# Windowed attention with sinks and a channel mix on one core: sink values as row tiles, 1 KB rows for q and k, longer filling, new orders

## The chip, the cores and the metric

The kernel runs on one core of one Trainium2 chip. The metric is the device time of one execution in microseconds; lower is better. A core has a matrix engine (TensorE, in profiles PE, with its weight loads shown as PEld), a vector engine (VectorE, DVE), an activation engine (ScalarE, ACT), a general engine (GpSimd, POOL) and SyncE (SP), which issues DMAs. Each engine works through its own queue in order and waits at semaphores for the others. Matmuls write to PSUM, in eight banks; everything else lies in SBUF, with 128 partitions.

## The reference, cut to what matters

Attention over 4 batches, 8 heads, 768 tokens and 64 elements per head, in which a query sees the first 4 tokens (the sinks) and the last 128, followed by a channel mix with squared ReLU and a sigmoid gate:

```python
scores = scale * np.matmul(q, k.transpose(0, 1, 3, 2))
keep = is_sink | in_window               # pos < 4, or 0 <= rel < 128
a = softmax(np.where(keep, scores, -1e9))
x = np.matmul(a, v)                      # heads side by side: B, S, 512
xk = mu_k * x + (1.0 - mu_k) * x_prev    # x_prev: one token earlier
xr = mu_r * x + (1.0 - mu_r) * x_prev
k = np.maximum(xk @ w_k, 0.0)            # 512 x 1024
v = k * k @ w_v                          # 1024 x 512
out = (1.0 / (1.0 + np.exp(-(xr @ w_r)))) * v
```

Inputs and output are float32.

## The kernel before, in words

The work is cut into 12 units of 256 tokens (4 batches, 3 units each; T is the unit's number in its batch). For each unit there are four stages.

`prepare` casts q and k to bf16 and transposes them, so that the 64 elements of a head lie on partitions (tiles qt and kt). One chunk c is a pair of heads, and a half is two chunks. For units in KD (k, from 4) and QD (q, from 8) SP issues a DMA transpose (L603); for the others PE transposes (L616) into a PSUM bank, and ACT or DVE evacuates it (L624). These "PE-transposed" units load q and k in rows of 512 B (L403: two neighbouring tokens of a head in one partition), a whole tensor of a unit by one DMA of 512 KB, for unit 0 by two of 256 KB. v, and q and k of the units transposed by DMA, are loaded in rows of 256 B (L386, L396). v is cast into vb, with a column of ones (L638). For the first unit of a batch `prepare` also gathers the sinks' keys (L655, ksink, on POOL) and the sinks' values (L661 on PE and L665 on DVE, vsink, in which row 32c + 4a + s has sink s for head a of chunk c).

`attend` has PE multiply keys by queries for two chunks at a time into the two tiles sc (L701, matmuls over 64 rows, the two heads of a chunk in the upper and the lower half of the array); ACT takes the exponential (L737, tile e); DVE sets what is out of the window to zero (L751). Scores against the sinks are one set of four matmuls of 32 columns each per unit (L678), their exponential is the tile es (L685), in which the four chunks lie on 32 partitions each. `values` (from L757) multiplies by v: for T > 0 and each group g of 128 tokens first one matmul es x vsink over 128 rows for both heads (L763, 128x130), then four of e x vb (L775, 128x65). A chunk's values lie in one PSUM bank. DVE takes the reciprocal of the sums (L788) and multiplies (L791, tile x).

`mix` transposes x on PE (L814), ACT or DVE evacuates it (L823, xt), DVE takes the difference to the token before (L841, td) and makes xk and xr (L852).

`ffn` of the unit before has PE multiply xk by w_k (L902, keys), ACT or DVE take the ReLU (L912, L916), DVE square it (L924, kk), PE multiply xr by w_r (L933), ACT take a tanh (L939), PE multiply kk by w_v (L951) and DVE join both (L960); SP stores (L967). The weights are loaded in float32 and cast (L552 to L558).

The order of the work is not left to a scheduler. The kernel first notes every operation in a list (`Plan.op`), with its engine, a cost, what it reads and writes and the buffers that it takes and holds. ORDER has the numbers of these operations for each engine, in the order in which that engine does them, and CHOICE names the engine for operations that may run on several. `Plan.schedule` walks these lists with the costs to assign buffers and to merge the engines; it also places zero matmuls (L971, on the tile `warm`) into the time in which PE has nothing to do by the plan's clock: where a gap is over 300 ns (600 ns before 4 us), a bank is free, and the plan's clock stands below `fill_until`, 22000 ns. In PSUM the pool "sc" has 2 tiles of two banks each and the pool "bank" has the other 4 banks. The plan allows 100 ns (SWITCH) where PE changes between kinds of tiling (mode 0 for the whole array, 1 for scores, 2 for sink scores); the cost of `values` is 358 ns for T > 0.

```python
for g in range(2):
    if T > 0:
        nc.tensor.matmul(out=o[:, g, :, :],
                         lhsT=buf["es", u][:, 128 * g:128 * g + 128],
                         rhs=vsink[b % 2][:, 2 * c:2 * c + 2, :],
                         start=True, stop=False, skip_group_check=True)
```

Of the kernel before, what the change touches and what calls it, by code (L numbers as in the profile page):

```python
# [18 lines left out]
    79: "ACT", 82: "ACT", 83: "ACT", 85: "ACT", 87: "ACT", 89: "DVE", 94: "DVE", 95:  # L19
    "DVE", 97: "DVE", 101: "DVE", 102: "DVE", 128: "DVE", 134: "DVE", 136: "DVE", 137:  # L20
    "DVE", 140: "ACT", 141: "DVE", 150: "DVE", 191: "DVE", 192: "ACT", 193: "ACT", 218:
    "DVE", 265: "DVE", 273: "DVE", 278: "DVE", 305: "DVE", 343: "DVE", 346: "DVE", 348:
    "DVE", 352: "ACT", 354: "DVE", 361: "DVE", 423: "DVE", 429: "ACT", 430: "ACT", 499:
    "DVE", 501: "DVE", 504: "DVE", 507: "DVE", 508: "ACT", 520: "DVE", 586: "ACT", 587:
    "ACT", 654: "DVE", 658: "DVE", 660: "DVE", 663: "DVE", 672: "DVE", 736: "DVE", 738:
    "ACT", 739: "DVE", 744: "DVE", 751: "DVE", 815: "DVE", 816: "ACT", 825: "DVE", 885:
    "DVE", 887: "DVE", 891: "ACT", 892: "ACT", 1003: "DVE",
# [13 lines left out]
TOGETHER = 2  # L41

SWITCH = 100.0
# [8 lines left out]
        90, 93, 106, 96, 99, 104, 117, 77, 109, 114, 132, 138, 142, 129, 125, 120, 156,  # L52
        135, 158, 149, 184, 190, 169, 236, 208, 209, 212, 213, 220, 221, 161, 166, 172,
        177, 216, 194, 181, 201, 217, 187, 238, 291, 299, 292, 295, 300, 303, 249, 304,
        226, 296, 241, 246, 307, 224, 228, 277, 232, 229, 252, 261, 233, 267, 257, 311,
        264, 284, 270, 312, 319, 344, 309, 315, 330, 316, 349, 367, 375, 368, 376, 322,
        371, 395, 327, 372, 333, 338, 397, 275, 353, 379, 360, 380, 383, 408, 385, 387,
        422, 388, 445, 453, 446, 454, 400, 427, 405, 475, 411, 416, 391, 431, 392, 457,
        438, 458, 449, 473, 486, 450, 463, 526, 530, 527, 531, 500, 538, 461, 505, 539,
        469, 510, 470, 554, 478, 483, 534, 494, 489, 535, 512, 565, 557, 465, 579, 466,  # L60
        542, 519, 544, 562, 550, 584, 573, 551, 588, 546, 568, 632, 602, 547, 603, 606,
        614, 607, 595, 630, 643, 615, 620, 610, 618, 611, 640, 635, 678, 682, 679, 683,
        664, 646, 690, 706, 708, 686, 651, 687, 691, 626, 671, 719, 711, 622, 627, 694,
        623, 761, 757, 765, 758, 762, 766, 722, 696, 741, 727, 716, 775, 785, 702, 750,
        769, 743, 770, 796, 703, 788, 793, 698, 773, 699, 817, 777, 781, 778, 782, 835,
        831, 839, 832, 836, 799, 840, 859, 861, 843, 804, 847, 844, 824, 855, 849, 869,
        864, 872, 856, 907, 915, 908, 851, 916, 852, 880, 875, 911, 893, 912, 919, 900,
        920, 935, 937, 923, 925, 931, 948, 932, 973, 940, 974, 981, 945, 982, 951, 977,
        959, 978, 956, 985, 927, 966, 986, 928, 991, 989, 1001, 1009, 1005, 1002, 1013,
        1006, 1014, 1010, 993, 1021, 997, 994, 998, 1017, 1019, 1022, 1029, 1025, 1030,  # L70
        1026,
    ),
    "DVE": (
        69, 70, 89, 94, 95, 101, 97, 108, 102, 113, 110, 115, 111, 78, 137, 105, 116, 119,
        128, 124, 144, 126, 121, 134, 122, 127, 136, 150, 145, 151, 152, 146, 153, 191,
        147, 160, 148, 165, 80, 81, 154, 171, 141, 176, 162, 163, 167, 173, 168, 178, 174,
        179, 155, 196, 197, 203, 198, 205, 204, 211, 218, 199, 223, 206, 207, 84, 240,
        245, 305, 200, 86, 242, 306, 243, 247, 215, 248, 256, 219, 88, 278, 251, 294, 298,
        279, 230, 253, 302, 254, 234, 258, 259, 280, 265, 343, 286, 348, 281, 282, 287,
        289, 346, 321, 288, 313, 326, 317, 273, 337, 290, 323, 332, 324, 328, 283, 329,  # L80
        334, 339, 335, 340, 370, 354, 276, 374, 355, 361, 358, 362, 382, 356, 378, 364,
        357, 363, 423, 389, 399, 404, 410, 401, 415, 406, 402, 366, 412, 417, 407, 418,
        413, 359, 365, 448, 433, 393, 434, 440, 435, 442, 441, 456, 460, 499, 482, 477,
        504, 452, 529, 501, 488, 507, 436, 493, 511, 437, 471, 479, 480, 484, 444, 485,
        495, 556, 496, 490, 541, 491, 443, 537, 558, 572, 514, 559, 561, 533, 467, 515,
        520, 563, 521, 564, 517, 567, 574, 522, 575, 516, 523, 590, 552, 569, 591, 570,
        518, 525, 548, 524, 654, 634, 593, 639, 597, 660, 599, 658, 592, 598, 605, 645,
        636, 641, 637, 642, 650, 600, 617, 601, 613, 666, 647, 594, 609, 648, 652, 710,
        653, 669, 663, 667, 693, 668, 712, 672, 673, 675, 674, 676, 713, 628, 681, 624,
        670, 736, 721, 715, 726, 723, 724, 677, 685, 728, 729, 689, 760, 717, 742, 718,  # L90
        764, 792, 787, 751, 768, 739, 744, 789, 790, 794, 745, 704, 795, 746, 772, 752,
        748, 803, 747, 754, 753, 755, 700, 819, 779, 783, 798, 820, 749, 822, 834, 800,
        756, 801, 838, 805, 806, 815, 863, 842, 868, 825, 826, 821, 846, 827, 865, 828,
        866, 870, 885, 857, 823, 879, 887, 871, 829, 874, 853, 876, 881, 882, 877, 910,
        830, 918, 895, 898, 914, 902, 896, 922, 903, 939, 904, 944, 897, 933, 950, 941,
        942, 946, 947, 952, 955, 953, 905, 957, 958, 899, 961, 962, 906, 968, 976, 963,
        970, 969, 929, 980, 964, 972, 988, 984, 1003, 965, 1004, 1008, 971, 1012, 1016,
        995, 999, 1023, 1031, 1027,
    ),
    "ACT": (  # L100
        67, 68, 92, 91, 98, 112, 107, 100, 118, 131, 123, 133, 143, 139, 130, 183, 189,
        164, 159, 185, 79, 157, 175, 170, 82, 140, 210, 222, 237, 214, 180, 186, 195, 202,
        182, 192, 188, 244, 239, 293, 83, 301, 193, 255, 227, 250, 85, 297, 308, 87, 225,
        260, 266, 262, 263, 269, 268, 285, 271, 341, 325, 320, 345, 310, 336, 331, 350,
        369, 377, 396, 373, 419, 403, 398, 381, 421, 384, 424, 409, 386, 414, 352, 426,
        447, 455, 428, 481, 476, 432, 497, 439, 429, 502, 459, 451, 474, 487, 464, 528,
        532, 430, 492, 462, 506, 540, 560, 555, 508, 578, 536, 513, 571, 576, 580, 581,
# [188 lines left out]
def kernel(  # L296
# [374 lines left out]
    def attend(u, rank):  # L671
# [16 lines left out]
        lo = 0 if T > 0 else 128  # L688
        width = 2 * (512 - lo)

        def scores(c):
            sck = ("sc", u, c)
            kt, qt, sc = buf["kt", u], buf["qt", u], buf[sck]
            jobs = [(kt[:, c, 0, :], 128, 384, qt[:, c, :, :]),
# [329 lines left out]
```

## Time and profile before

| What | us |
|---|---|
| three runs | 170.58, 171.35, 173.37 |
| median | 171.35 |
| profiled execution: span from the first to the last instruction | 172.5 |
| busy: PE / PEld / DVE / ACT / POOL | 160.6 / 106.3 / 153.6 / 129.2 / 13.4 |
| share of the chain that ended last: PE / DVE / DMA / ACT | 82% / 10% / 3% / 2% |

The page gives no time of the profiled execution other than its span. Busy is the time in which an engine had at least one instruction at work. Matmuls and DVE's operations overlap their neighbours (a matmul of 512 columns lasts 0.38 us, but one starts every 0.216 us), so that where work is summed up, the spacing between the starts of neighbours in the timeline is used, not the duration. "The chain of waits" is the chain of work that ended last, followed back from the last instruction to what released each step. An engine's name with q is its queue, which issues DMAs. The granted clock is the share of TensorE's full clock that the chip allowed it.

### The profile page before, as it was taken

The page shows a single profiled execution, that of the slowest core. Times are in us where ns is not written, and L with a number is a line of the kernel's source. Part 1 is how long each engine was busy: PE and PEld are TensorE (multiplying, and loading weights), DVE is VectorE, ACT ScalarE, POOL GpSimd, SP SyncE. Part 2 cuts the span into 40 slices and gives each one's busy share as a digit, 9 for nine tenths or more (in the row PEclk, how much of TensorE's full clock was granted, in tenths as well). Part 3 has the DMA queues.
Part 4 walks back from the last instruction along what each step waited for, and adds up shares of the span by engine and source line. Part 5 has one row for each costly group of instructions (what it writes and reads, how often), then busy time and mean ns, then how long its engine had stood idle before and what let it go on. Part 6 is the DMA issues. An engine that isn't in the chain of part 4 may idle for free.

```text
span 172.5 us, 4178 instructions
## 1 busy us (share of the span) xinstructions
PE 160.6 (93%) x1588; PEld 106.3 (62%) x1605; DVE 153.6 (89%) x404; ACT 129.2 (75%) x208; POOL 13.4 (8%) x32
## 2 busy tenths in 40 slices
PE   7986869799999999999999999999999997999992
PEld 2444547675647667777567786756476773777551
DVE  6279895999999999999999999999999999699542
ACT  2488895999898999898979987865838958853320
POOL 7330000000010010050000200120000000000000
PEclk9999678999999999999999999999999999999999
DMA  4999999999156969999679489869969857102033
GB/s 144 243 302 365 291 254 353 380 298 229 26 139 157 287 124 240 197 257 289 163 170 226 96 212 243 159 170 212 240 149 256 213 111 211 61 4 113 11 122 122
DMA packets 81763, 33.82 MB, mean 196 GB/s; under 512 B 63688, under 2 KB 76240, under 8 KB 81744
## 3 DMA queue, kind: packets, MB, share of 16 engines
q1 hardware_dynamic: 81728, 33.56, 78.0%
q8 instruction: 12, 0.20, 0.6%
q14 instruction: 7, 0.06, 0.1%
q10 hardware_dynamic: 16, 0.00, 0.0%
HBM read 24.12 MB, written 6.29 MB: 176 GB/s over the span
## 4 chain that ended last, share of the span: by engine, by line
PE 82%; DVE 10%; DMA 3%; ACT 2%; issue 1%; DVEq 0%; ACTq 0%
PE bank L951 23%; PE bank L902 23%; PE bank L933 12%; PE sc L701 6%; PE bank L775 6%; PE bank L971 4%; PE bank L814 3%; DMA kt<-kb 3%; DVE e L751 2%; PE bank L616 2%; PE bank L763 2%; DVE xk L852 2%; ACT rl L912 1%; ACT e L737 1%; DVE x L791 1%
## 5 line engine op out<-in xcount | busy, mean ns | idle before, releaser
L902 PE MATMUL bank<-xk,wk_sb 128*128 128x256 bf16 x384 | 52.0, 278 | 1.6 <-DVE wk_sb L558 1.3
L737 ACT ACTIVATE e<-sc 128x1024 bf16<-128x1024 f32 (+1 forms) x48 | 44.5, 964 | 4.0 <-PE sc L701 4.0
L951 PE MATMUL bank<-wv_h,kk 128*128 128x512 bf16 x174 | 44.9, 379 | 0.7 <-issue 0.3
L902 PEld LDWEIGHTS <-wk_sb 128*128 128x128 bf16 x384 | 36.1, 100 | 10.2 <-DVE wk_sb L558 1.6
L912 ACT ACTIVATE rl<-bank 128x512 bf16<-128x512 f32 x45 | 26.2, 608 | 12.2 <-PE bank L902 9.6
L751 DVE TENSOR_TENSOR e<-e,mask 128x1024 bf16<-128x1024 bf16 (+1 forms) x48 | 30.0, 637 | 0.7 <-ACT e L737 0.7
L951 PEld LDWEIGHTS <-kk 128*128 128x128 bf16 x184 | 16.7, 98 | 15.8 <-issue 0.7
L933 PE MATMUL bank<-wr_sb,xr 128*128 128x512 bf16 x89 | 23.6, 379 | 0.3
L852 DVE SCALAR_TENSOR_TENSOR xk<-td,mu_all,xt 128x256 bf16<-128x256 bf16 x48 | 22.4, 491 | 0.1
L852 DVE SCALAR_TENSOR_TENSOR xr<-td,mu_all,xt 128x256 bf16<-128x256 bf16 x48 | 22.4, 476 | 0.0
L939 ACT ACTIVATE th<-bank 128x512 f32<-128x512 f32 x24 | 14.7, 618 | 7.8 <-PE bank L933 7.7
L960 DVE SCALAR_TENSOR_TENSOR ob<-th,bank 128x512 f32<-128x512 f32 x23 | 15.6, 680 | 5.6 <-ACT th L939 3.5
L791 DVE TENSOR_TENSOR x<-bank,rec 128x256 bf16<-128x256 f32 x48 | 19.4, 416 | 0.4
L924 DVE TENSOR_TENSOR kk<-rl 128x512 bf16<-128x512 bf16 x48 | 19.4, 415 | 0.1
L775 PE MATMUL bank<-vb,e 128*128 128x65 bf16 x352 | 18.9, 193 | 0.2
L775 PEld LDWEIGHTS <-e 128*128 128x128 bf16 x352 | 16.4, 98 | 3.0 <-DVE e L751 0.7
L701 PE MATMUL sc<-qt,kt 64*128 64x128 bf16 (+1 forms) x256 | 15.0, 246 | 1.7 <-DMA kt<-kb 0.9
L701 PEld LDWEIGHTS <-kt 64*128 64x128 bf16 x256 | 9.4, 97 | 7.9 <-issue 3.4
L933 PEld LDWEIGHTS <-xr 128*128 128x128 bf16 x96 | 8.9, 98 | 8.5 <-issue 0.3
L763 PE MATMUL bank<-vsink,es 128*128 128x130 bf16 x64 | 12.4, 220 | 0.4 <-ACT rl L912 0.3
L823 ACT COPY xt<-bank 128x512 bf16<-128x512 bf16 x15 | 8.8, 586 | 5.3 <-PE bank L814 5.1
L788 DVE RECIPROCAL rec<-bank 128x4 f32<-128x4 f32 x48 | 8.0, 174 | 3.2 <-ACT rl L912 1.8
(67 smaller groups left out, 166.5 us busy)
## 6 DMA issues: line engine op xcount, KB each, us to landing
vs<-in_v_dram SPq DMA_DIRECT2D x24, 256.0 KB, 3.9
out_dram<-ob SPq DMA_DIRECT2D x23, 256.0 KB, 3.2
ks<-in_k_dram SPq DMA_DIRECT2D x18, 256.0 KB, 4.7
qs<-in_q_dram SPq DMA_DIRECT2D x7, 512.0 KB, 9.5
qs<-in_q_dram SPq DMA_DIRECT2D x10, 256.0 KB, 5.4
w<-in_moe_w_k_dram SPq DMA_DIRECT2D x2, 1024.0 KB, 9.2
w<-in_moe_w_v_dram SPq DMA_DIRECT2D x2, 1024.0 KB, 9.9
ks<-in_k_dram SPq DMA_DIRECT2D x3, 512.0 KB, 8.0
```

The lines of the kernel that those rows point to most:

```text
L701: nc.tensor.matmul(out=sc[:, a, o0:o1], lhsT=lhs[rows], rhs=rhs[rows], start=u not in BIAS, stop=True, skip_group_check=u in BIAS)
L737: nc.scalar.activation(out=buf[ek][:, :, lo:], in_=buf[sck][:, :, lo:], func=AF.Exp, scale=scale)
L751: nc.vector.tensor_tensor(out=at, in0=at, in1=m, op=ALU.mult)
L763: nc.tensor.matmul(out=o[:, g, :, :], lhsT=buf["es", u][:, 128 * g:128 * g + 128], rhs=vsink[b % 2][:, 2 * c:2 * c + 2, :], start=True, st ...
L775: nc.tensor.matmul(out=o[:, g, a, :], lhsT=e[:, a, e0:e0 + 128], rhs=rhs, start=(T == 0 and i == 0), stop=(i == len(blocks) - 1), skip_gro ...
L791: P.op("DVE", dve(256), lambda ok=ok, rk=rk, c=c: nc.vector.tensor_tensor(out=buf["x", u][:, :, 128 * c:128 * c + 128].rearrange("p g (a d ...
L852: nc.vector.scalar_tensor_tensor(out=buf[key][:, c0 + i, :], in0=buf[tk][:, i, :], scalar=mu[w][:, c0 + i:c0 + i + 1], in1=xt[:, c0 + i, t ...
L902: nc.tensor.matmul(out=ps[:, i, :], lhsT=wk_sb[:, c, 128 * f:128 * f + 128], rhs=xk[:, c, :], start=(c == 0), stop=(c == NC - 1), skip_gro ...
L912: nc.scalar.activation(out=buf[rk], in_=buf[psk].rearrange("p (i t) -> p i t", i=2), func=AF.Relu)
L924: P.op("DVE", dve(512, 0.52), lambda f2=f2, rk=rk: nc.vector.tensor_tensor(out=buf["kk", u][:, 2 * f2:2 * f2 + 2, :], in0=buf[rk], in1=buf ...
L933: nc.tensor.matmul(out=buf[psk], lhsT=buf["xr", u][:, c, 128 * g:128 * g + 128], rhs=wr_sb[:, c, :], start=(c == 0), stop=(c == NC - 1))
L951: nc.tensor.matmul(out=buf[psk], rhs=wv_h[:, f, :], lhsT=buf["kk", u][:, f, 128 * g:128 * g + 128], start=(f == 0), stop=(f == NF - 1))
```

## The change

It has five parts.

- Sink values: for T > 0 two chunks are done together, in `sink_values`, ahead of `values`: one matmul over 64 rows for each chunk and group, the two chunks in the two halves of the array, each into its own bank. To that end the chunks are taken in the order 0, 2, 1, 3 (CHUNK), since es has chunks 0 and 1 in the upper 64 partitions and 2 and 3 in the lower. The operation takes both banks and has the same mode as the scores.
- q and k of the PE-transposed units: four neighbouring tokens of a head in one partition, rows of 1 KB, by two DMAs, each into 64 partitions. Casts, transposes and evacuations take the new layout; their numbers stay.
- `fill_until` goes from 22000 to 32000.
- CHOICE is new: 16 casts of q, k and v stand on POOL instead of 3; on ACT there are 21 casts of q and k instead of 32, and 19 evacuations of q and k instead of 17; on DVE 13 casts of q and k instead of 16, and 5 evacuations instead of 7.
- ORDER is new for every engine. The halves of x's transposes are now chunks 0 and 2, and 1 and 3.

In the built kernels PE has 24 zero matmuls before and 23 after: 13 ahead of the first transposes before, 11 after; in the new one a zero matmul stands directly ahead of the first scores of unit 1 and another behind the first scores of unit 2; in the old one none stands behind the scores of unit 0.

```diff
+CHUNK = (0, 2, 1, 3)
...
-            P.op("SP", 400.0 + 20.0 * (h1 - h0), lambda key=key, src=src: nc.sync.dma_start(
-                out=buf[key][:, h0:h1, :, :].rearrange("p h j d -> p h (j d)"),
-                in_=src[b, h0:h1, 256 * T:256 * T + 256, :].rearrange(
-                    "h (p j) d -> p h (j d)", j=2)), rank,
-                service=128 * (h1 - h0) * 1.96 + 45.0, descs=128 * (h1 - h0), take=[] if h0 else [(name + "s", key)],
-                hold=[key] if h0 else [],
-                writes=[(name, u, hp) for hp in range(h0 // 4, h1 // 4)])
+            rows = src[b, :, 256 * T:256 * T + 256, :].rearrange(
+                "(w l) (p j) d -> w p l (j d)", w=2, j=4)
+            c0, c1 = h0 // 4, h1 // 4
+            for w in range(2):
+                P.op("SP", 400.0 + 20.0 * (c1 - c0), lambda key=key, rows=rows, w=w: (
+                    nc.sync.dma_start(
+                        out=buf[key][64 * w:64 * w + 64, h0:h1].rearrange(
+                            "p (l x) j d -> p l (x j d)", x=2),
+                        in_=rows[w][:, 2 * c0:2 * c1])), rank,
+                     service=128 * (c1 - c0) * 3.33 + 45.0, descs=128 * (c1 - c0),
...
             def transpose(half=half, psk=psk, rk=rk):
-                ps = buf[psk].bitcast(BF16)[:, 0:512].rearrange("p (c j t) -> p c j t", c=2, j=2)
-                for i in range(2):
-                    for j in range(2):
-                        c = 2 * half + i
-                        nc.tensor.transpose(
-                            out=ps[:, i, j, :], identity=ident,
-                            in_=buf[rk][:, j, 2 * c:2 * c + 2, :].rearrange("p a d -> p (a d)"))
+                ps = buf[psk].bitcast(BF16)[:, 0:512].rearrange("p (j t) -> p j t", j=4)
+                for j in range(4):
+                    nc.tensor.transpose(
+                        out=ps[:, j, :], identity=ident,
+                        in_=buf[rk][:, half, 2 * j:2 * j + 2, :].rearrange("p a d -> p (a d)"))
...
                 return lambda: copy(
-                    out=buf[key][:, 2 * half:2 * half + 2, :, :].rearrange(
-                        "p c g (t j) -> p c j (g t)", j=2),
+                    out=buf[key][:, half::2, :, :].rearrange(
+                        "p c g (t j) -> p c j (g t)", j=4),
...
+                if T > 0:
+
+                    def sink_values(cs=cs):
+                        for g in range(2):
+                            for r, i in enumerate(cs):
+                                rows = slice(64 * r, 64 * r + 64)
+                                o = buf["o", u, i][:, 130 * g:130 * g + 130]
+                                nc.tensor.matmul(
+                                    out=o.rearrange("p (a d) -> p a d", a=2),
+                                    lhsT=buf["es", u][rows, 128 * g:128 * g + 128],
+                                    rhs=vsink[b % 2][rows, 2 * CHUNK[i]:2 * CHUNK[i] + 2, :],
+                                    start=(g == 0), stop=False, skip_group_check=True)
+
+                    P.op("PE", 114.0, sink_values, r + 1, lag=PE_LAG, mode=1,
+                         take=[("bank", ("o", u, i)) for i in cs], hold=[("es", u)],
+                         writes=[("os", u, i) for i in cs], reads=[("es", u), ("vsink", b % 2)])
...
                 for g in range(2):
-                    if T > 0:
-                        nc.tensor.matmul(out=o[:, g, :, :],
-                                         lhsT=buf["es", u][:, 128 * g:128 * g + 128],
-                                         rhs=vsink[b % 2][:, 2 * c:2 * c + 2, :],
-                                         start=True, stop=False, skip_group_check=True)
                     for a in range(2):
...
-            P.op("PE", 358.0 if T else 180.0, values, r + 1, lag=PE_LAG, take=[("bank", ok)],
-                 hold=[ek, ("vb", u)] + ([("vb", u - 1), ("es", u)] if T else []), writes=[ok],
+            P.op("PE", 232.0 if T else 176.0, values, r + 1, lag=PE_LAG,
+                 take=[] if T else [("bank", ok)],
+                 hold=[ek, ("vb", u)] + ([("vb", u - 1), ok] if T else []), writes=[ok],
...
-    P.fill_until = 22000.0
+    P.fill_until = 32000.0
```

CHOICE and ORDER, tables of numbers, are left out of the diff; what they move is in the list above.

## The prediction

> **What bounds the kernel now.** I read the page's 40 slices first, then busy time by stage, then the chain of waits in order of time, then the timelines of PE, DVE and POOL. The slices (each 4.3 us, tenths):
>
> ```profile
> PE   7986869799999999999999999999999997999992
> DVE  6279895999999999999999999999999999699542
> PEclk9999678999999999999999999999999999999999
> ```
>
> Until slice 7 PE and DVE both have holes, and in slices 4 to 6 the granted clock of TensorE falls; from slice 9 both are full. By stage (stretch, its length, then busy us of PE, PEld, DVE, ACT and POOL, granted clock, DMA share, GB/s):
>
> ```profile
> 15.00:30.00 15.00, 11.83 (x132) 8.70 (x133) 12.33 (x33) 12.19 (x20) 0.00 (x0) 0.77 1.07 312
> 36.00:140.00 104.00, 102.97 (x1081) 68.95 (x1094) 103.23 (x271) 87.67 (x143) 7.46 (x9) 1.00 0.86 195
> 146.00:170.00 24.00, 23.20 (x194) 15.32 (x194) 17.17 (x42) 10.83 (x19) 0.00 (x0) 1.00 0.18 66
> ```
>
> Between 36 and 140 us PE and DVE are both busy for 99% of the time: neither can be relieved alone. After 146 PE alone works off what is left. So time can be won in the first 35 us, at a PE wait near 142, or by relieving PE and DVE together.
>
> The chain of waits (start, length, what):
>
> ```profile
> 1.13 5.73 PE bank L971 x13
> 24.36 3.45 PE bank L902 x16
> 59.43 0.55 PE sc L701 x12
> 59.98 0.97 PE bank L933 x4
> 60.95 0.86 PE bank L951 x4
> 139.08 4.50 DMA kt<-kb
> ```
>
> Thirteen zero matmuls (0.44 us each) stand ahead of the first transposes. Sixteen key matmuls take 3.45 us at 24.36, where sixteen take 1.75 us elsewhere in the chain (52.59): the clock there is half. Four 512-column matmuls take 0.86 us, but 0.97 behind score matmuls, which work on 64 rows: changing the tiling costs about 0.1 us. Twelve scores take 0.55, and their six pairs need 2 x (0.109 + 2 x 0.056) = 0.44 at the spacing of starts; so 0.1 again on the way in. From the spacing of PE's starts the exact figure is 0.094 each way.
>
> DVE pays for the half clock: it waits 1.84 us for the values of unit 1, which stand behind those sixteen matmuls in PE's queue.
>
> ```profile
> 26.16 0.68 DVE L751 TENSOR_TENSOR e<-e,mask 128x1024 bf16<-128x1024 bf16 x1
> 28.68 0.18 DVE L788 RECIPROCAL rec<-bank 128x4 f32<-128x4 f32 x1 [1.84 <-ACT rl L912]
> ```
>
> **The change part by part.** The sum is against the profiled execution: span 172.5 us (the page gives no other time of it), 1.15 above the median of the runs, 171.35.
>
> *Sink values as row tiles.* Now 64 matmuls of 128x130 (L763), one start every 0.057 us:
>
> ```profile
> 27.64 0.22 PE L763 MATMUL bank<-vsink,es 128*128 128x130 bf16 x1
> 27.70 0.28 PE L775 MATMUL bank<-vb,e 128*128 128x65 bf16 x4
> ```
>
> 64 x 0.057 = 3.6 us. As pairs in two row tiles, which start 4 ns apart in the scores of the trace, they take 32 x 0.06 = 1.9: -1.7 us. But a tile group that doesn't stand next to scores switches the array there and back. In the built instruction order PE's changes of tiling rise from 59 to 75: 16 x 0.094 = +1.5. Net -0.2; ends -1.7 (no switch felt) and +1.5 (pairs don't overlap). The group also takes two of the four banks before the values need them; that cost is in the ends.
>
> The Trainium skill, TensorEngine Tiling (Array Packing), section Key Properties, says that changing the tiling mode drains the array and gives no price. By its silence the gain would be 1.7; by the row above it is nearly nothing.
>
> *q and k in 1 KB rows.* Units 0 to 2 load six tensors of 1024 packets of 512 B before steady work. The trace's packets last 28 to 29 ns at 512 B and 89 at 2048, so 1024 B lies near 49: 6 x (1024 x 29 - 512 x 49) / 16 = 1.7 us less DMA time. The high end is the cost per byte of the 256 B rows, 20 ns: 80 ns per KB, +4.2 us. I take 49, but a gain of nothing: between 13 and 36 us no wait of PE, DVE or ACT over 0.5 us ends with a load; what covers a later landing is DVE's full queue. Each load becomes two issues on SP, each for one half of the partitions: 14 more, at 0.35 (a store) to 0.5 us. In the steady part SP's own waits cover them (66 us in the list of its queue's waits, some 25 of them in the tail). At the start they show: the first k half is complete with the third issue, not the first, q with the fourth, not the second, so both land some 0.9 us later (casts at 4.8 and 5.6 instead of 3.87 and 4.72).
>
> The Trainium skill, SBUF — State Buffer, section Door 1, says that 64 partitions reach 8 of 16 ports, with 196 GB/s measured against 328, and the next section that two such transfers serialize. By it 1 KB would take about 98 ns (estimate from that page) and the start-up loads 7.7 us more; no transfer of this trace goes to 64 partitions.
>
> *Fewer zero matmuls first, more later.* 11 instead of 13 stand ahead of the first transposes, so these start at 1.13 + 11 x 0.44 = 6.0 instead of 6.65, with q's cast (now on DVE behind k's) done at 6.0: -0.6. Ends: -0.9, and +0.4 if eight transposes then run at half clock. The longer limit places only two or three after 15 us. The clock fell after 12 to 17 us with PE 36 to 78% busy; 0.2 us of filling hardly lifts that, so I keep the half clock.
>
> *Orders and engines.* Up to the first mask of unit 1 (now 22.02) DVE's work at the spacing of starts is 15.5 us, after the change 16.4; its waits are 6.5. Of these, the two evacuation waits shrink with the earlier transposes, and the 0.59 at 18.04 goes, since the x transposes stand ahead of the unit's scores: I count 4.5. So 20.9: 1.1 ahead, the 0.6 included. Then nine DVE operations (4.5 us) reach 25.4 to 25.9, among them a relu and two v casts that now lie where DVE waited. The last key group ahead of the values waits for a weight cast on ACT near 23.3; with 8 key matmuls at half clock the values come at 25.3. So the reciprocal runs at 26.0, not 28.68. Start-up sum: -2.6; ends 0 (PE later by as much) and -4.3 (clock full: 3.45 becomes 1.75).
>
> *Casts on POOL.* ACT loses eleven casts (11 x 0.51 us at the spacing of starts, off the bound). DVE's own work falls by 2.0 us in all, 2.4 after unit 2. POOL casts rise from 3 to 16. They disturb DVE:
>
> ```profile
> 32.29 1.27 DVE L852 SCALAR_TENSOR_TENSOR xk<-td,mu_all,xt 128x256 bf16<-128x256 bf16 x3
> ...
> 61.45 1.62 DVE L852 SCALAR_TENSOR_TENSOR xk<-td,mu_all,xt 128x256 bf16<-128x256 bf16 x3
> 61.59 0.81 POOL L638 CAST vb<-vs 128x512 bf16<-128x512 f32 x1 [13.28 <-DMA vs<-in_v_dram]
> ...
> 73.76 2.44 POOL L655 COPY ksink<-kt 64x16 bf16<-64x16 bf16 x2 [11.36 <-DMA kt<-kb]
> ```
>
> Three equal operations take 0.35 us more beside one POOL cast, as much as DVE's own cast occupies it (0.34). Two tiny copies take 2.44 us when DVE is dense, 0.5 otherwise: POOL waits. Nine of the new casts fall after unit 1: 9 x 0.35 - 2.4 = +0.7. Ends -2.4 (no disturbance) and +2.1 (all thirteen). Queued behind them on POOL are sink keys and the next casts; SP waits with DMA transposes for four of them (units 5, 6, 11), with loads and stores behind. The loads run ahead of need; their late landing is what shows first.
>
> *The wait at 142.* PE waits 1.1 us for the last k transposes. The new order issues them behind a POOL cast but with other orders of SP; I take -1.0, ends -1.1 and +1.1 (twice as long).
>
> Kernel-wide, PE's work at the spacing of starts, switches and zeros included, is 151.6 before and 151.2 after; 22.2 us of it follow the last scores in both, so the tail stays.
>
> Sum: -0.2 - 2.6 + 0.7 - 1.0 = -3.1: span 169.4, time 168.2.
>
> **Rivals.** *Full clock* (0.20): the start's lead reaches 4.3 and POOL's disturbance is covered: 166.0. For it: the new transposes and zeros lie in the weak stretch; against it: few of them. *Lead given back* (0.16): units 2 and 3 find ACT or banks late, or DVE's disturbance takes 2 us more: 171. For it: equal PE work, DVE 99% busy. *Slow half loads* (0.12): rows at 80 ns or worse: instead of the lead, 4.2 us later weights and keys: 172.5 + 4.2 = 176.7, time 175.5. It decides from about +3.5 us on the start. *POOL late* (0.10): each of nine casts is held as at 73.76 (2.4 us) and PE waits 0.94 as at 142: 9 x 0.94 - 3.8 = +4.7, time 176. It takes eight of nine to be over 2% slower. *The change doesn't do what it says*: only the longer filling can be so, and it is priced at nothing.
>
> **How the numbers follow.** The forecast, 168.2, has 0.42; its own range is 166.5 to 170.5. A measurement of this kernel can tell about 2% from no change, so the bounds are 167.9 and 174.8. Of the 0.42, 0.24 fall below 167.9; with the full clock, faster is 0.44. The rest of it and the returned lead make 0.34 for no change; the two late rivals 0.22. The range leaves out the worse half of the slow cases and the best of the full clock: 164.8 to 175.6.
>
> **What would show it.** Right: first transposes at 6.0; reciprocal of unit 1 near 26; scores followed by 0.97-us groups, and sink groups too, with L763's successor 0.12 us for four matmuls; DVE operations lengthened by 0.35 beside POOL casts; PE over 98% from 36 on. Wrong: granted clock 1.00 through slices 4 to 6 (full clock); PE waiting for DMA or kb after 36 (POOL late); ks and qs landing later than 5 us for 256 KB (slow halves); DVE with waits in the middle while PE is full.

## The result, and the profile after

The changed kernel takes 178.93 us (median of 4 runs, 177.17 to 179.77), the kernel before 171.5 beside it: a ratio of 1.043 (95% interval 1.036 to 1.050), 7.4 us slower. Forecast were 168.2 us and a range up to 175.6; the time lies outside, on the other side of no change. The profiled execution took 178.37 us with a span of 176.7, so 1.67 us lie around the span. The two profiled spans are only 4.2 us apart (176.7 and 172.5); the last paragraph on why the prediction was wrong says why. Here and below a ratio compares fast runs alone (a run over 1.5% above the fastest of its kernel is left out) while a median holds all runs, so the two can differ.

The 40 slices of the changed kernel (4.4 us each):

```profile
PE   7883866899989999999999999999999999999992
DVE  5578998999979999899999999998999899997851
PEclk9999699999999999999999999999999999999999
```

The forecast wanted PE full from 36 us on. PE has a hole as late as slice 12, DVE in slices 12, 17, 28 and 32. The clock is no longer the trouble: one slice is lowered where three were. By stage (length, busy us of PE, PEld, DVE, ACT and POOL, clock, DMA share, GB/s):

```profile
36.00:140.00 104.00, 101.80 (x1052) 65.52 (x1050) 99.54 (x253) 92.31 (x143) 11.54 (x17) 1.00 1.00 207
```

ACT has 4.6 us more to do here than before (92.31 against 87.67), although eleven of its casts went to POOL; DVE falls from 103.23 to 99.54 and PE from 102.97 to 101.80: both now wait, and PE's 97.9% of this stretch misses the 98% that the forecast named. The page's chain by engine, and two of its groups:

```profile
PE 56%; ACT 16%; DVE 14%; SPq 5%; DMA 4%; issue 3%; POOL 0%; DVEq 0%; POOLq 0%
...
L639 ACT COPY qt<-bank 128x512 bf16<-128x512 bf16 x13 | 17.4, 1336 | 3.2 <-PE bank L631 3.2
...
L639 ACT COPY kt<-bank 128x512 bf16<-128x512 bf16 x6 | 7.7, 1324 | 4.2 <-PE bank L631 4.1
```

The same two groups of the kernel before:

```profile
L624 ACT COPY qt<-bank 128x512 bf16<-128x512 bf16 x11 | 8.3, 757 | 0.2 <-PE bank L616 0.2
L624 ACT COPY kt<-bank 128x512 bf16<-128x512 bf16 x6 | 4.4, 737 | 2.2 <-PE bank L616 2.2
```

The evacuations of q and k copy as many elements as before, out of the same kind of bank into the same kind of tile, and take 1.33 us instead of 0.75. In shape and type the two rows are equal. What differs is where the writes go, which no column shows: before, a run of 128 bf16 of the bank goes to every second place of the tile (4 bytes apart), now a run of 64 to every fourth (8 bytes apart), since four tokens of a head lie in one partition. On DVE it is 1.30 us instead of 0.73 (5 of them).

The second thing that is new stands at the start of the chain (start, length, what):

```profile
8.49 0.62 SPq L418
9.15 0.61 SPq L418
9.81 6.47 DMA ks<-in_k_dram
...
16.40 0.62 POOL kb L606
17.07 0.58 PE bank L631 x4
17.68 1.30 DVE kt L639
```

Unit 1's k is issued at 9.81 and is there 6.47 us later; a cast on POOL, the transposes and an evacuation hang on it. The trace's packets of 1024 bytes, nearly all of them these loads into the 64 lower or upper partitions, take 72.8 ns on the mean, 79 where they follow each other in 11 to 17 us. Before, a KB in two packets of 512 bytes took 62, and 67 in 11 to 17 us. From 11 to 15 us the DMA engines move 231 GB/s, 315 before, and are busy in both.

DVE after the change at unit 1, to be held against the two rows that the forecast showed (mask 26.16, reciprocal 28.68):

```profile
28.40 0.69 DVE L782 TENSOR_TENSOR e<-e,mask 128x1024 bf16<-128x1024 bf16 x1
29.11 0.42 DVE L815 RECIPROCAL rec<-bank 128x4 f32<-128x4 f32 x2
```

The reciprocal was to run at 26.0 and runs at 29.11: 0.43 us behind the kernel before, and 3.5 us more are lost by the end (PE's last matmul starts at 172.98 instead of 169.03).

### The profile page after: what moved, and what is told of

It reads as the page before. It is cut to its first block, busy times and chain, and to the rows that moved or that the text cites. A ratio compares the mean times of both kernels' runs of the same rounds, so it can differ in the third digit from the quotient of the medians.

```text
span 176.7 us, 4240 instructions
## 1 busy us (share of the span) xinstructions
PE 161.3 (91%) x1604; PEld 103.4 (59%) x1604; DVE 157.2 (89%) x399; ACT 134.7 (76%) x200; POOL 19.7 (11%) x45
## 4 chain that ended last, share of the span: by engine, by line
PE 56%; ACT 16%; DVE 14%; SPq 5%; DMA 4%; issue 3%; POOL 0%; DVEq 0%; POOLq 0%
PE bank L979 16%; PE bank L930 16%; PE bank L961 8%; ACT qt L639 5%; PE bank L801 5%; ACT e L768 5%; PE sc L716 4%; SPq L418 4%; DMA ks<-in_k_dram 4%; DVE xr L879 3%; DVE kk L952 2%; PE bank L841 2%; DVE e L782 2%; ACT kt L639 2%; PE bank L756 2%
## 5 line engine op out<-in xcount | busy, mean ns | idle before, releaser
L930 PE MATMUL bank<-xk,wk_sb 128*128 128x256 bf16 x384 | 51.1, 273 | 2.5 <-ACT wk_sb L568 1.8
L768 ACT ACTIVATE e<-sc 128x1024 bf16<-128x1024 f32 (+1 forms) x48 | 45.6, 981 | 3.2 <-PE sc L716 3.0
L979 PE MATMUL bank<-wv_h,kk 128*128 128x512 bf16 x184 | 46.3, 379 | 0.0
L930 PEld LDWEIGHTS <-wk_sb 128*128 128x128 bf16 x384 | 35.5, 98 | 13.2 <-issue 2.2
L952 DVE TENSOR_TENSOR kk<-rl 128x512 bf16<-128x512 bf16 x48 | 20.1, 432 | 0.5 <-ACT rl L940 0.4
L639 ACT COPY qt<-bank 128x512 bf16<-128x512 bf16 x13 | 17.4, 1336 | 3.2 <-PE bank L631 3.2
L801 PE MATMUL bank<-vb,e 128*128 128x65 bf16 x352 | 16.2, 193 | 2.2 <-DVE e L782 2.2
L801 PEld LDWEIGHTS <-e 128*128 128x128 bf16 x352 | 13.9, 97 | 5.4 <-DVE e L782 2.3
L850 ACT COPY xt<-bank 128x512 bf16<-128x512 bf16 x16 | 9.5, 596 | 2.2 <-PE bank L841 2.1
L639 ACT COPY kt<-bank 128x512 bf16<-128x512 bf16 x6 | 7.7, 1324 | 4.2 <-PE bank L631 4.1
```

The costliest lines, as they stand in the source:

```text
L639: return lambda: copy(out=buf[key][:, half::2, :, :].rearrange("p c g (t j) -> p c j (g t)", j=4), in_=buf[psk].bitcast(BF16)[:, 0:512].re ...
L768: nc.scalar.activation(out=buf[ek][:, :, lo:], in_=buf[sck][:, :, lo:], func=AF.Exp, scale=scale)
L801: nc.tensor.matmul(out=o[:, g, a, :], lhsT=e[:, a, e0:e0 + 128], rhs=rhs, start=(T == 0 and i == 0), stop=(i == len(blocks) - 1), skip_gro ...
L930: nc.tensor.matmul(out=ps[:, i, :], lhsT=wk_sb[:, c, 128 * f:128 * f + 128], rhs=xk[:, c, :], start=(c == 0), stop=(c == NC - 1), skip_gro ...
L952: P.op("DVE", dve(512, 0.52), lambda f2=f2, rk=rk: nc.vector.tensor_tensor(out=buf["kk", u][:, 2 * f2:2 * f2 + 2, :], in0=buf[rk], in1=buf ...
L979: nc.tensor.matmul(out=buf[psk], rhs=wv_h[:, f, :], lhsT=buf["kk", u][:, f, 128 * g:128 * g + 128], start=(f == 0), stop=(f == NF - 1))
```

## Theories

*Theory 1*: the stride of the evacuations, on ACT and DVE. *Theory 2*: the loads of q and k into 64 neighbouring partitions. *Theory 3*: the new orders, with the sink values in row tiles and POOL's casts. Ratios below are to runs of the kernel before on the same chip; the runs are spread over three chips, so differences of medians between runs are rough. The diffs are shortened, with ... for what is left out.

## Experiment 1: each half of the layout undone alone, and both

`a_evac2` undoes the stride alone:

```diff
-  "p c g (t j) -> p c j (g t)", j=4),  in_= ... "p (j c t) -> p c j t", c=2, j=4
+  "p c g (t j) -> p c j (g t)", j=2),  in_= ... "p (c j t) -> p c j t", c=2, j=2
```

> The changed kernel with one line undone: the evacuations of the transposed q and k write every second bf16 (4 bytes apart) as the kernel before does, in place of every fourth (8 bytes apart). Loads, casts, orders and sink matmuls stay as changed. The tokens then stand permuted in the transposed q and k, so the scores belong to other pairs; the amount of work is the same. Theory 1 (the evacuations' stride: 19 on ACT at 1.33 us instead of 0.75, 5 on DVE at 1.30 instead of 0.73, and they now stand on the chain): evacuations back to 0.75 us, their share of the chain from 5% to 1% or less, time 171 to 173.5 us. Theory 2 (the q and k loads, 73 to 79 ns a packet of 1 KB): evacuations faster, but the time falls by under 2 us, 176.5 to 178.5. Theory 3 (the new orders and POOL's casts): as theory 2.

Measured: 176.3 us, ratio 1.0225 (1.017 to 1.029). The evacuations take 0.75 us again, yet only 2.6 of 7.4 us come back.

`a_rows512_evac4` undoes the loads alone (casts and transposes follow the rows; only the load is shown):

```diff
-  out=buf[key][64 * w:64 * w + 64, h0:h1].rearrange("p (l x) j d -> p l (x j d)", x=2),
-  in_=rows[w][:, 2 * c0:2 * c1]
+  out=buf[key][:, hw].rearrange("p h j d -> p h (j d)"),     # hw: heads of this DMA
+  in_=src[b, hw, ...].rearrange("h (p j) d -> p h (j d)", j=2)
```

> The changed kernel with only the loads of q and k put back to rows of 512 bytes over all 128 partitions (still two DMAs a load, four heads each; casts and transposes follow the old raw layout); the evacuations keep their 8-byte stride, so the tokens stand permuted and the scores belong to other pairs, with the same amount of work. Theory 1 (evacuations): the packets fall from 73 to about 31 ns each (62 per KB), the key of unit 1 lands some 2 us earlier, but the time stays within 2 us of the changed kernel, 176.5 to 178.5. Theory 2 (loads): 172 to 174, first mask of unit 1 back from 24.4 to under 22. Theory 3 (orders): 177 to 179.

Measured: 178.2 us, ratio 1.0355 (1.030 to 1.041). The packets are back at 30 ns per 512 bytes, and the time is the changed kernel's within 0.7 us; the two intervals overlap.

`a_old_layout` has both edits:

> The changed kernel with the whole layout of q and k undone: rows of 512 bytes over 128 partitions, casts, transposes and evacuations as in the kernel before; the new orders, the sink values as two row tiles, POOL's casts and the longer filling stay. Theory 1 (evacuations): 170 to 173 us, no more than 1 us better than with the stride alone undone. Theory 2 (loads): 170 to 172, and at least 3 us better than with the stride alone undone. Theory 1 and 2 together (say 5 us and 2 us): 169 to 171.5, near what the prediction wanted without its layout terms. Theory 3 (the orders, the row tiles or POOL's casts cost the time): 175.5 to 178.5.

Measured: 171.49 us, ratio 0.9942 (0.991 to 0.998). Alone, the two edits give 2.6 and 0.7 us; together 7.4. By the ratios, each to its own chip, it is 2.1% and 0.8% against 4.9%. Theory 3 falls: with the old layout the new orders, row tiles and POOL's casts are no slower than the kernel before. Theories 1 and 2 fall as each was stated, since I had them compete; they hold together. Where the time of `a_evac2` goes, by stage and in its chain:

```profile
36.00:60.00 24.00, 20.19 (x217) 12.65 (x218) 20.75 (x51) 18.18 (x30) 4.25 (x7) 1.00 1.10 227
```

```profile
36.57 0.60 SPq L418
...
37.22 13.66 DMA ks<-in_k_dram x2
50.88 0.41 DVE xk L879
```

```profile
45.01 0.74 POOL L606 CAST kb<-ks 128x512 bf16<-128x512 f32 x1 [7.61 <-DMA ks<-in_k_dram]
45.79 0.23 PEld L631 LDWEIGHTS <-kb 128*128 128x128 bf16 x4 [1.43 <-POOL kb L606]
45.80 0.40 PE L631 MATMUL bank<-ident,kb 128*128 128x128 bf16 x4 [1.26 <-POOL kb L606]
```

With fast evacuations PE is idle for 3.8 of these 24 us, and the keys of units 3 and 4 land late: POOL waits 7.61 us for a load, PE then 1.26 us for POOL, and the chain from 37.22 to 50.88 is loads of keys. PE's other waits here (0.9 and 0.8 us for DVE, 0.5 for a weight cast on ACT) were not followed back to a load one by one. With fast loads and slow evacuations (`a_rows512_evac4`) PE is idle for 2.1 us of the same stretch (21.92 busy) and 1.0 of the next 20, and ACT makes 22% of its chain. Both costs stand in front of the same transposed q and k. Whichever is left is then the later one, so to take away one shows little of it: this reading of the two chains fits the sums above.

## Experiment 2: why the loads are slow, and the evacuations' walk turned round

`a_spread_rows` keeps rows of 1 KB and 64 partitions a DMA, but takes every second partition:

```diff
-  out=buf[key][64 * w:64 * w + 64, h0:h1]
+  out=buf[key][w::2, h0:h1]
```

> The changed kernel with its q and k loads in the same 1 KB rows, but each DMA's 64 rows go to every second partition (one to the even, one to the odd ones) in place of the lower or upper 64. The tokens then stand in another order and the scores belong to other pairs, with the same amount of work. If what makes a 1 KB packet take 73 ns (79 back to back) is that one DMA writes only 64 neighbouring partitions: packets fall to 47 to 55 ns, the key of unit 1 lands about 2 us earlier, and the time falls by 0 to 2 us, to 176 to 178. If 1 KB rows or two DMAs at once are slow by themselves: packets stay at 70 to 80 ns and the time within 0.7 us of 178.4.

Measured: 177.69 us, ratio 1.032 (1.027 to 1.037). Packets take 50.5 ns from 11 to 15 us, and the rate is 350 GB/s. So neither 1 KB rows nor two DMAs are slow by themselves: the neighbouring 64 partitions are. The forecast's 49 ns would have been right for this form. The time moves by 1.2 us, as theory 1 needs: the evacuations are left.

`a_gather` turns the walk of the evacuation round:

```diff
-  out= ... "p c g (t j) -> p c j (g t)", j=4),  in_= ... "p (j c t) -> p c j t", c=2, j=4
+  out= ... "p c g (t j) -> p c (g t) j", j=4),  in_= ... "p (j c t) -> p c t j", c=2, j=4
```

> The changed kernel with only the order in which an evacuation walks its tile changed: it writes 1 KB of neighbouring bf16 in order and takes them from the bank at strides of 256 bytes, where it took neighbours and wrote every fourth. What is computed is the same. If the stride of the writes into SBUF makes 1.33 us: back to 0.75 us or less, and the time as with the stride undone, 175.5 to 177 (the loads still stand on the chain there). If any strided side costs as much: 1.2 to 1.4 us and 177.5 to 179.5.

Measured: 176.19 us, ratio 1.030 (1.026 to 1.035). Its rows for q on ACT and DVE, and two rows of the kernel before for the evacuation of x, which reads and writes neighbours:

```profile
L639 ACT COPY qt<-bank 128x512 bf16<-128x512 bf16 x13 | 7.7, 593 | 4.1 <-PE bank L631 4.1
L639 DVE COPY qt<-bank 128x512 bf16<-128x512 bf16 x3 | 2.1, 686 | 0.5 <-PE bank L631 0.5
...
L823 ACT COPY xt<-bank 128x512 bf16<-128x512 bf16 x15 | 8.8, 586 | 5.3 <-PE bank L814 5.1
L823 DVE COPY xt<-bank 128x512 bf16<-128x512 bf16 x9 | 3.7, 416 | 0.6 <-PE bank L814 0.6
```

Neighbours written, the bank read at steps of 256 bytes: 0.59 us on ACT (0.69 on DVE), less than the 0.75 of the kernel before. So the walk of the writes in SBUF makes the 1.33 us. On ACT the stride in the bank then costs nothing against the copy of x, which has no such stride on either side (0.59); on DVE it still costs 0.27 us (0.69 against 0.42). No run separates the stride of the writes from the shorter runs that come with it (64 places instead of 128). The time is as with the stride undone, since the loads are left.

`a_spread_gather` has both and keeps 1 KB rows:

```diff
-  out=buf[key][64 * w:64 * w + 64, h0:h1]
+  out=buf[key][w::2, h0:h1]
...
-  "p c g (t j) -> p c j (g t)", j=4),  in_= ... "p (j c t) -> p c j t", c=2, j=4
+  "p c g (t j) -> p c (g t) j", j=4),  in_= ... "p (j t c) -> p c t j", c=2, j=4
```

> The changed kernel with both costs that the runs have shown taken away and its 1 KB rows kept: the loads go to every second partition (packets of 49 to 55 ns where 64 neighbouring partitions made 73 to 79), and the evacuations write neighbouring bf16 and take them from the bank at a stride. What is computed is the same. Theory (either cost alone holds the time at 176 to 178, because loads and evacuations feed the same waits of TensorE, and only both together give it back): 169.5 to 172.5, if the strided reads cost no more than 0.8 us each. If the strided reads cost as the strided writes did: 177 to 178.5. Rival (something else of the 1 KB layout costs time, not loads and evacuations): 174 or more though both are fast.

Measured: 171.47 us, ratio 1.000 (0.996 to 1.004). This is the changed kernel with what it set out to do, 1 KB rows and all, without its two costs:

```profile
20.00:28.00 8.00, 6.12 (x88) 4.29 (x87) 8.00 (x22) 7.60 (x12) 0.61 (x1) 1.00 0.95 268
36.00:60.00 24.00, 23.91 (x244) 14.92 (x243) 23.91 (x65) 21.40 (x36) 4.50 (x7) 1.00 1.08 255
```

```profile
26.71 0.29 DVE L815 RECIPROCAL rec<-bank 128x4 f32<-128x4 f32 x2
```

PE and DVE are full again from 36 to 60 us, and unit 1's reciprocal runs at 26.71 (26.15 in a second profile of this kernel, `s_base` below). The 1 KB rows themselves are worth nothing here: `a_old_layout` has the same time.

## Experiment 3: each cost alone on the kernel before

Two edits of experiment 1 are put into the kernel before, each alone: in `b_evac4` the walk with `j=4`, in `b_half_rows` the two DMAs of 64 neighbouring partitions, issued one behind the other:

```diff
-  nc.sync.dma_start(out=buf[key][:, h0:h1, :, :], ...)
+  for w in range(2):
+      nc.sync.dma_start(out=buf[key][64 * w:64 * w + 64, h0:h1].rearrange(
+          "p (l x) j d -> p l (x j d)", x=2), in_=rows[w][:, h0 // 2:h1 // 2])
```

> The kernel before with only its evacuations of q and k changed to write every fourth bf16; tokens stand permuted, so the scores belong to other pairs, with the same amount of work. Loads, orders and all else stay. Theory (the stride alone holds the time at 176 to 178 in either order): evacuations 1.30 to 1.34 us, 17 on ACT and 7 on DVE for 24, 175 to 178.5, against 172.5 for the kernel before. Rival (the old order has slack for it, and only the new orders expose it): under 174.

Measured: 179.04 us, ratio 1.047 (1.042 to 1.052), evacuations 1.30 to 1.33 us. The stride alone makes the kernel before as slow as the changed one, 0.5 us over the theory's range.

> The kernel before with only its q and k loads changed: each is two issues, one for the lower and one for the upper 64 partitions, in rows of 1 KB; heads and tokens then stand in another order and the scores belong to other pairs, with the same amount of work. Orders, evacuations and all else stay. Theory (loads into 64 neighbouring partitions take 72 to 79 ns a packet and alone hold the time at 175.5 to 177.5, as the evacuations alone hold it at 176 to 179): 175 to 177.5, packets 70 to 79 ns, chain with 10% or more of DMA and SP's queue. Rival (the old orders start earlier with the loads and have slack): packets the same, time under 174.

Measured: 174.53 us, ratio 1.0185 (1.011 to 1.026); packets 70 ns, 77 from 11 to 17 us. The old orders cover part of it: 2.7 us, where in the changed kernel 4.7 stand between `a_gather` and `a_spread_gather`. The time is 0.5 us under the theory's range and over the rival's, and the chain has 8% of DMA and SP's queue, not 10%.

`b_gather` and `a_old_gather` turn the walk round where a stride of 4 bytes was, in the kernel before and in `a_old_layout`:

```diff
-  "p c g (t j) -> p c j (g t)", j=2),  in_= ... "p (c j t) -> p c j t", c=2, j=2
+  "p c g (t j) -> p c (g t) j", j=2),  in_= ... "p (c j t) -> p c t j", c=2, j=2
```

> The kernel before with only the walk of its evacuations of q and k changed: neighbouring bf16 written in order, taken from the bank at a stride of 256 bytes. What is computed is the same. The runs so far had 0.59 us for such a copy on ACT and 0.69 on DVE, where this kernel's every-second write takes 0.75 and 0.73. 17 on ACT at 0.15 and 7 on DVE at 0.04: 2.6 us of ACT's time and 0.3 of DVE's. If the evacuations still end waits of TensorE at a stride of 4 bytes: 0.5 to 2 us faster. If at 0.75 us they are already covered: within 0.5 us of the kernel before.

Measured: 172.24 us beside 171.85, ratio 0.996 (0.992 to 1.001): no difference is shown.

> The changed kernel with the layout of q and k as in the kernel before (171.5 us beside 172.5) and, on top, evacuations that write neighbouring bf16 in order and take them from the bank at a stride. What is computed is the same. Theory (the evacuations are covered once they take 0.75 us or less): within 0.6 us of the same without the new walk, ratio to the kernel before 0.99 to 0.998. Rival (each tenth still counts): ratio 0.98 to 0.99.

Measured: 171.55 us, ratio 0.997 (0.993 to 1.001). At 0.75 us the evacuations are covered; at 1.33 they are not. Of the versions tried, `a_old_layout` alone lies below the kernel before with its whole interval, by 0.6%.

## Experiment 4: the forecast's smaller terms

`before_again` is the kernel before, profiled once more.

> The kernel before once more, for a second profile beside the first, whose span of 172.5 us stands above what its times allow (171.9 median less 1.7). If the first profile is a late execution: a span of 169 to 171, with the difference at the start-up's half clock; then 1 to 3 us of what the prediction took as the start-up's lead and the wait at 142 was in the execution and not in the kernel. If the span is 172 or more, the rest of the change is worth its 3 us and the time outside the span differs.

Measured: 172.75 us, span 171.1, so 1.65 us lie around the span. It is between the two cases of the expectation, and the clock at the start is no higher than in the first profile. There is no wait of PE near 142 in this execution (PE's list of waits is empty from 138 to 146 us). The reciprocal of unit 1 runs at 28.40, the clock from 20 to 28 us is 0.62:

```profile
20.00:28.00 8.00, 6.18 (x40) 4.18 (x40) 6.11 (x12) 5.63 (x9) 0.00 (x0) 0.62 1.05 268
```

The three others change one thing each of `s_base`, which is `a_spread_gather` again (same chip, 12 runs each).

> The reference for the three beside it: the changed kernel with loads to every second partition and evacuations that write neighbouring bf16 (171.5 us before, ratio 1.000 to the kernel before). Expected ratio 0.993 to 1.003, 170.6 to 172.4 us.

Measured: 171.93 us, ratio 0.998 (0.994 to 1.003).

`s_full_sinks`:

```diff
-  rows = slice(64 * r, 64 * r + 64)
+  rows = slice(0, 128)
```

> s_base with the sink values' matmuls over all 128 rows again. Prediction's term (row tiles -0.2 us): ratio to the kernel before within 0.003 of s_base's. Rival (the row tiles gain nearly all of the 1.7 us, and the changes of tiling cost little): ratio 0.006 to 0.012 above s_base's.

Measured: 172.84 us, ratio 1.003 (0.999 to 1.007). The same edit on the old layout, beside `a_spread_gather` (1.000) on its chip:

> The changed kernel with the whole layout of q and k as in the kernel before, and the sink values' matmuls over all 128 rows again, two a pair in place of two half-height ones; orders, POOL's casts and filling stay. Against the same with row tiles (171.5 us): the prediction has the row tiles at -0.2 us in all (less matmul time, 16 more changes of tiling). Theory (the row tiles are nearly free either way): 171 to 172.3. Rival (the changes of tiling cost more than 0.094 us each): 0.8 us or more faster, under 170.7. Rival (the row tiles gain all their 1.7 us): 172.5 or more.

Measured: 171.94 us, ratio 1.005 (1.001 to 1.009). The row tiles look 0.5% better than the full matmuls both times (1.1% beside `a_old_layout`, on another chip), between the two cases expected for `s_full_sinks`; on one chip the intervals overlap.

`s_casts_on_dve` renames fourteen entries of CHOICE and moves their numbers from POOL's list to DVE's:

```diff
-    109: "POOL", 112: "POOL", 142: "POOL", 148: "POOL", ...
+    109: "DVE", 112: "DVE", 142: "DVE", 148: "DVE", ...
```

> s_base with its fourteen casts that had been put on POOL (q, k and v) moved to DVE, each where the planner's time of its start falls in DVE's order. DVE takes about 14 x 0.34 = 4.8 us more of its own work, POOL 9 us less. Prediction's view (a cast on POOL costs DVE as much as its own, 0.35 us): within 0.6 us of s_base. If POOL's casts are nearly free: 1.5 to 5 us slower than s_base. If they hold DVE and SP's transposes for longer (POOL late): 1 to 3 us faster.

Measured: 173.01 us, ratio 1.005 (1.001 to 1.009), 1.1 us above `s_base`, again between the cases expected, and the intervals overlap.

```diff
-    P.fill_until = 32000.0
+    P.fill_until = 22000.0
```

> s_base with zero matmuls placed in planned waits up to 22 us again instead of 32. Prediction's view (the longer filling is worth nothing): within 0.5 us of s_base, the granted clock of 20 to 36 us within 0.05 of s_base's. Rival (the longer filling is what keeps the clock up there): clock of 20 to 30 us down to 0.8 or less, 0.8 us or more slower.

Measured: 171.62 us, ratio 0.996 (0.992 to 1.000), with the clock at 1.00 from 20 to 36 us in both. The longer filling is worth nothing, as forecast.

## Why the prediction was wrong

*The step that failed first is one that the forecast doesn't have.* It counted the evacuations as moved (19 instead of 17 on ACT, in the list of the change), but its sum has no term for them: their cost stood at nothing, without a reason, as if the same shape meant the same duration. The diff changed their access pattern, and at the spacing of starts that costs 0.44 us each on ACT (1.03 instead of 0.59) and 0.47 on DVE (1.09 instead of 0.62): 19 x 0.44 + 5 x 0.47 = 10.7 us of engine time. Alone on the kernel before it makes 7.2 us. A bound from both sides for "the same copy at twice the write stride" would have put it on the list of unknown costs: no row of the trace had a stride of 8 bytes. The trace did have a hint. The evacuations of x (L823, experiment 2) and of q are equal in shape and type too, x without a stride, and at 4 bytes q already took 0.17 us more on ACT (0.76 against 0.59) and 0.31 on DVE (0.73 against 0.42):

```profile
L624 DVE COPY qt<-bank 128x512 bf16<-128x512 bf16 x5 | 3.6, 725 | 3.2 <-PE bank L616 3.2
```

*"I take 49"* for a packet of 1 KB was wrong for these loads: 72.8 on the mean, 79 back to back, the forecast's own high end. "What covers a later landing is DVE's full queue" failed with it; from 36 to 60 us POOL and then PE wait for keys (experiment 1). The rival *slow half loads* had the mechanism, and its +4.2 us is near the 4.7 that the loads cost once the evacuations are fast; but it was given 0.12, and it was priced alone; on the kernel before the loads cost 2.7. Its sign came: 256 KB of q or k land 5.3 and 5.6 us after their issue (medians of the page), where over 5 was to show it. The forecast set the Trainium skill's rule (SBUF — State Buffer, section Door 1: 64 neighbouring partitions reach half of the ports) beside the rows and took the rows, none of which went to 64 partitions. The measured 231 GB/s against 350 for the same bytes to every second partition is the rule's direction; the forecast's estimate of 98 ns from it was too high, 79 is what came.

*The start-up* came near its numbers, with luck in it. First transposes: forecast 6.0, measured 5.92; but with the old orders they start at 6.65, 5.74, 5.53 and 5.28 (`before`, `before_again`, `b_evac4`, `b_gather`), since the thirteen zero matmuls ahead of them last 5.73, 4.78, 4.56 and 4.32 us there. So no gain from two fewer is shown: the executions differ by as much. Reciprocal of unit 1: forecast 26.0, measured 26.15 and 26.71 once both costs are away; `b_gather` has it at 26.76 with the old orders, whether through its faster evacuations or by the execution is not shown. One reason was wrong: "I keep the half clock". The clock from 20 to 28 us is 0.96 in the changed kernel and 0.99 to 1.00 in its variants (0.62 to 0.77 with the old orders), and not through the longer filling, since the short one has it too. What keeps it up stays open.

*The wait at 142*, -1.0, belonged to one execution of the kernel before and not to its order: `before_again`, `b_gather`, `b_evac4` and `b_half_rows` have none there.

*Casts on POOL*, +0.7, priced like casts on DVE (0.35 against 0.34 us), were priced too high as far as one profile each shows: DVE's 376 operations other than casts last 169.7 us in sum in `s_base` and 169.3 with fourteen casts moved to DVE, so beside POOL's casts they lose some 0.4 us in all, not 14 x 0.35 = 4.9. Moved to DVE, the casts raise its busy time by 3.7 us (152.6 to 156.3); the times lean the same way, by 1.1 us, but their intervals overlap. *Sink values*, -0.2: by the spacing of starts in `s_base` and `s_full_sinks`, a group of row tiles that stands alone costs PE 0.09 us more than four full matmuls, and one beside the matmuls of the attention scores 0.10 or more less; there are eight of each, so the sum is small, as forecast. The times lean to a larger gain, which stays unsettled.

*The sum.* Without the layout's costs the rest is worth 0 to 1.0 us, not 3.1. One us of the difference is the wait at 142. Beyond that, the profiled execution (span 172.5, so some 174.2 us) was 2.3 us slower than the median of 171.9. The forecast took it to be 1.15 above, since it set the span against the median of the times. Its span of 169.4 came true to the digit in `a_old_layout`, whose profiled execution took 171.09 us and not 168.2; that is a coincidence, since it is another kernel and the sum has terms that were wrong. Part of what the forecast saw to be won was thus in the one execution that it read. The reciprocal is some 2 us ahead of both profiles of the kernel before, yet the medians show no more than 1, and `b_gather`, 1.6 to 1.9 ahead, shows none clear of noise; where the remainder is given back I did not settle.

## What to carry to other kernels

Where a diff changes a layout, price every instruction that reads or writes it anew, also those whose shape and number stay: the stride stands in no column of the profile. A trace can hold the same copy with and without a stride: hold the two against each other first. On ACT, let a copy that has to reorder write neighbours and read at a stride from the bank; on DVE that is better than writing at 8 bytes too, but not free. And where two suspects feed the same wait, undo both before either is acquitted: here they gave 2.6 and 0.7 us alone and 7.4 together.

## What the runs showed of the hardware that was not expected

A copy of 128x512 bf16 from a bank into SBUF on ACT takes 0.59 us when it writes neighbours, 0.75 at a write stride of 4 bytes and 1.33 at 8, and it is 0.59 whether the bank is read in order (the copy of x) or at steps of 256 bytes (`a_gather`). On DVE it is 0.42 in order on both sides, 0.69 with the strided read, 0.73 and 1.30 with the strided writes: there each stride costs. The Trainium skill (Advanced Engine Details and Errata, section SBUF Cachelines) asks for two hits on a line of 16 bytes for full speed; a stride of 8 bytes has two bf16 on each such line, and these runs, for writes, don't agree (1.33 us against 0.59).

A DMA into 64 partitions moves 1 KB rows at 50 to 51 ns a packet from 11 to 15 us if it takes every second partition (`a_spread_rows`, `a_spread_gather`, `s_base`), and at 76 to 79 there if it takes 64 neighbours (the changed kernel, `a_evac2`, `a_gather`, `b_half_rows`).
